# Query weights and expert rows loaded in quarters in a gated mix of an S4 convolution and a PEER mixture of experts

## The chip, the cores and the metric

One Trainium2 chip, one of its cores. The metric is the device time of one execution in microseconds; runs of one kernel are given by their median. TensorE (PE) does the matmuls, with its weight loads (PEld) beside them; VectorE (DVE), ScalarE (ACT) and GpSimd (POOL) work element by element; SyncE (SP) issues nearly all DMAs, in the order in which they stand in its program.

## What is computed

Two layers on the same 2048 tokens of 576 channels, mixed by a gate. Layer A is a long convolution, whose kernel comes from 128 complex states per channel, made by FFT; layer B picks, for each token and each of 32 heads, two of 4096 experts by the scores of two halves of a query.

```python
g = sigmoid((x * gate_w).sum(-1, keepdims=True))
K = einsum("dn,dnl,dn->dl", Cc, exp(logdA[:, :, None] * l), dB).real
a = irfft(rfft(x padded) * rfft(K padded))[:L] + x * Dskip
q = einsum("nd,dhc->nhc", x, w_q)              # 32 heads, 2 x 128
s1, s2 = q[..., :128] @ k1.T, q[..., 128:] @ k2.T   # 64 scores each
two best of s1, two best of s2 -> two best of the four sums, softmax
b = sum over heads, k of softmax * gelu(x . u[expert]) * v[expert]
out = g * a + (1 - g) * b
```

## The kernel before

The program is written out by generators that one planner interleaves. `clock[0]` is the planner's time of TensorE; `spawn` puts a generator into a heap, `yield t` asks to be resumed t microseconds later, and `pump` (line 220) resumes what is due. `rdy` holds the time at which the planner expects each tile, `dma` (line 200) adds a transfer to `wire[0]`, the time at which all transfers so far would have passed. So a `yield` is no instruction: it only decides where in the order of the engines' programs the next instruction is put. On the chip every engine runs its own list in order and waits by semaphores.

Three streams share TensorE up to the last stage. Groups `s{c}_{t}` (128 of them, 14 matmuls of 512 columns) give the scores of the 512 key columns of block c for token tile t; VectorE takes the eight best and their indices from PSUM (`scores_top`, line 952). Groups `a{c}_{tb}_{j}` (128, 14 matmuls each) give x . u for 512 experts; ScalarE or VectorE copies each to `go` and SyncE stores it to `g_d` (`act_post`, 1378). The third stream makes the convolution: `u_stage1` (1063, matmuls `u`, in 16 pieces `u1_0` to `u1_15`) transforms the input, `k_params`, `k_front`, `k_gen` (matmuls `kP`, `kb`) build the kernel K in 36 chunks; when both have ended, `freq` (1265) loads the tables `tk` and the stored chunks `ksb`, `k_stage1` (1134, matmuls `k`) and `products` (1164, matmuls `pr`, `pi`, `pv`) follow. The main loop (1725 to 1765) takes the next `s` group if its weights are there and VectorE isn't too far behind, else the next `a` group; the last 26 `a` groups are kept back as long as the next `s` block has its weights. When all groups are through, `gating` (981) gives the transposes `tr`, `prep` (1498) builds the expert weights `wh` from one-hots (matmuls `S`), and the last stage multiplies them with the values `vhl` (matmuls `o`).

Block c of the scores needs its query weights folded with the keys: `w_next` (664) loads half a block (`w_load`, tile `wq{c}_{h}`, 128 x 2304 floats, in one DMA), `w_half` (598) squares it on ScalarE, sums the squares by a matmul `wn`, folds by the matmuls `wb` and splits the result into two halves of 16 bits, `whl` and `wrem`. Block c of the experts needs `uhl`: `u_build` (1323) loads 512 expert rows by `u_load` (1309): tile `us{c}`, 128 x 4 x 512 floats, in one DMA and then the last 64 of the 576 channels twice as two short DMAs (tile `ur{c}`); `squares` (442) squares both on ScalarE and sums by a matmul `sq`, and four splits follow. Both kinds of load take the one token `raw` (`quota`, line 288) and hold it until their block is built; a second token is there from the end of `u_stage1` on.

```python
        yield from need("raw")
        take("raw", "raw")
        yield from need("slot")
        w_load(c, h)
        yield from w_half(c, h, wl[c, h])
```

Of the kernel before, what the change touches and what calls it, by code (L numbers as in the profile page):

```python
# [12 lines left out]
F32 = mybir.dt.float32  # L13
# [11 lines left out]
D = 576  # L25
# [113 lines left out]
def body(ctx: ExitStack, tc: tile.TileContext, xT, au, par, logdt, dskip, gatew, wq, kT, uT, vv,  # L139
# [17 lines left out]
    def key(x):  # L157
        n = x.tensor.name
        return (n, x.offset) if n in columns else n

    def size(x):
        n = 1
        for d in x.shape[1:]:
            n *= d
        return n
# [34 lines left out]
    def dma(o, i, q=None):  # L200
        t = max(clock[0], rdy.get(key(i), 0.0), queue[0])
        queue[0] = t + 0.45
        wire[0] = max(wire[0], t) + (2 if o.dtype in (F16, BF16) else 4) * o.shape[0] * size(o) / 3.4e5
        rdy[key(o)] = max(rdy.get(key(o), 0.0), wire[0] + 2.2)
        (q or DQ).dma_start(o, i)
# [29 lines left out]
    def ready(*xs, late=0.0):  # L235
        while True:
            t = max(rdy.get(key(x), 0.0) for x in xs) + late - clock[0]
            if t <= 0:
                return
            yield t  # L240
# [20 lines left out]
    def need(tag, n=1):  # L261
        while True:
            lst = sorted(slots[tag])
            if len(lst) >= n and lst[n - 1] <= clock[0]:
                return
            yield max(0.2, lst[n - 1] - clock[0]) if len(lst) >= n else 0.3

    def take(tag, name):
        lst = slots[tag]
        assert lst, name  # L270
        lst.remove(min(lst))

    def free(tag, *outs):
        if owed[tag]:
            owed[tag] -= 1
            return
        slots[tag].append(max([clock[0]] + [rdy.get(key(x), 0.0) for x in outs]))
# [108 lines left out]
    def slot(shape, dt, name):  # L386
        take("slot", name)
        return bp.tile([128] + shape, dt, tag="s", name=name, bufs=9)
# [35 lines left out]
    def halves_load(a, src, c):  # L424

        columns.add(a.tensor.name)
        for m in (0, 2):
            dma(a[:, m:m + 2], src[128 * m:128 * m + 256, c].rearrange("(k p) n -> p k n", p=128))
# [71 lines left out]
    def scale_first(a, r, sq, keep=None):  # L500

        acc = [newcol() for _ in range(3)]
        yield from ready(r)
        S.activation(sq[:, 4], r, AF.Square, accum_out=sc[:, acc[0]])
        for n, m in enumerate((0, 2)):
            yield from ready(a[:, m:m + 2])
            S.activation(sq[:, m:m + 2], a[:, m:m + 2], AF.Square, accum_out=sc[:, acc[n + 1]])
        yield from ready(sq)
        yield from need("kb")
        p = bank("kb", "sq")  # L510
        for n in range(3):
            mm(p[:, 0:1], onesb, short(acc[n].start, 1), n == 0, n == 2, 0.05)
        yield from ready(p)
        out = root_scale(p[:, 0:1], 1.02)
        if keep is not None:
            V.tensor_copy(keep, p[:, 0:1])
        free("kb", out[0])
        return out
# [43 lines left out]
    whl, wl, sk, halves, scaled = {}, {}, [], {}, []  # L562
    side = lambda: "kb" if caps["wb"] == 0 else "wb"

    def w_load(c, h):
        a = slot([4, D], F32, f"wq{c}_{h}")
        g = 8 * c + 4 * h
        dma(a, wq[:, g:g + 4, :])
        wl[c, h] = a
# [28 lines left out]
    def w_half(c, h, w):  # L598
        fl = lambda x: x.rearrange("p a b -> p (a b)")
        yield from ready(w)  # L600
        pbs = []
        if c == 0:
            spawn(fold_first(h, w, pbs))
        while 1 not in scaled:
            yield 0.2
        acc = newcol(True), newcol(True)
        junk = wj.tile([128, 2, D], BF16, tag="wj", name=f"wj{c}_{h}")
        for n in range(2):
            S.activation(fl(junk), fl(w[:, 2 * n:2 * n + 2]), AF.Square, accum_out=sc[:, acc[n]])
        yield from ready(junk)  # L610
        while not sk:
            yield 0.3
        tag = side()
        yield from need(tag)
        p = bank(tag, f"wn{c}_{h}")
        for n in range(2):
            mm(p[:, 0:1], onesb, short(acc[n].start, 1), n == 0, n == 1, 0.03)
        yield from ready(p)
        s, i = root_scale(p[:, 0:1], kk, True)
        V.tensor_copy(invW[:, 2 * c + h:2 * c + h + 1], i)  # L620
        free(tag, s)
        while c not in halves:
            yield 0.3
        hl, rem, count = halves[c]
        o = slice(256 * h, 256 * h + 256)
        if c:
            yield from w_fold(c, h, w, pbs, (side(),) * 3)
        while not pbs:
            yield 0.2
        for k, tag, pb in pbs:  # L630
            spawn(w_tail(c, k, pb, hl, rem, o, count, s, tag), 0.3 * k)
        del pb, pbs
        free("slot")
        if c > 0:
            free("raw")
        if h == 0 and c > 0:
            spawn(w_next(c, 1))
        elif h == 1 and c < 7:
            spawn(w_next(c + 1, 0))
# [24 lines left out]
    def w_next(c, h):  # L664
        while sdone[0] < c - (kdone[0] == NCK) and 8 * NT - len(groups) < NT * c - 5:
            yield 0.3
        yield from need("raw")
        take("raw", "raw")
        yield from need("slot")
        w_load(c, h)  # L670
        yield from w_half(c, h, wl[c, h])

    def w_build(c):
# [635 lines left out]
    def u_load(c):  # L1309
        a = slot([4, 512], F32, f"us{c}")  # L1310
        r = actp.tile([128, 512], F32, tag="ur", name=f"ur{c}")
        cs = slice(512 * c, 512 * c + 512)
        if c:
            dma(a, uT[0:512, cs].rearrange("(k p) n -> p k n", p=128))
        dma(r[0:64], uT[512:576, cs])
        dma(r[64:128], uT[512:576, cs])
        if c == 0:
            halves_load(a, uT, cs)
        return a, r

# [2 lines left out]
    def u_build(c):  # L1323
        while adone[0] < c - (kdone[0] < NCK or sdone[0] >= 7):
            yield 0.3
        if c:
            yield from need("raw")
            take("raw", "raw")
            yield from need("slot")
        a, r = xl.pop("u") if c == 0 else u_load(c)  # L1330
        if c:
            yield from ready(a, r)
        yield from need("slot")
        hl = slot([2, 4, 512], F16, f"uhl{c}")
        sq = hl.rearrange("p a k n -> p (a k) n")[:, 0:5].bitcast(BF16)
        if c == 0:
            first_u[0] = hl
            s, i = yield from scale_first(a, r, sq, nu[:, 0:1])
            marks["s"].append(1)
        else:  # L1340
            yield from squares(a, r, sq, nu[:, c:c + 1])
            s, i = root_scale(nu[:, c:c + 1], 1.02)
        if len(xb) == 4:
            V.tensor_scalar(i_a[:, c, :], i_x, i, None, op0=OP.mult)
        else:
            i_u[c] = i
        rem = wrems[c % 2]
        if c == 0:
            for k in range(4):
                S.activation(hl[:, 0, k, :], a[:, k, :], AF.Copy, scale=s)  # L1350
                marks["h"].append(S.free + 0.28)
            S.activation(rem[:, 0, :], r, AF.Copy, scale=s)
            marks["h"].append(S.free + 0.28)
        for k in range(4):
            if c:
                yield from split(hl[:, 0, k, :], hl[:, 1, k, :], a[:, k, :], s)
                continue
            while 0 not in scaled:
                yield 0.1
            rdy[key(hl)] = marks["h"][k]  # L1360
            V.scalar_tensor_tensor(hl[:, 1, k, :], a[:, k, :], s, hl[:, 0, k, :], op0=OP.mult, op1=OP.subtract)
            marks["u"].append(V.free + 0.28)
        if c:
            S.activation(rem[:, 0, :], r, AF.Copy, scale=s)
        yield from ready(rem)
        V.scalar_tensor_tensor(rem[0:64, 1, :], r[0:64], s[0:64], rem[0:64, 0, :], op0=OP.mult, op1=OP.subtract)
        if c == 0:
            marks["u"].append(V.free + 0.28)
        free("slot", hl)
        free("raw", hl)  # L1370
        uhl[c] = hl, rem
        yield from ready(rem)
        while len(scaled) < 4:
            yield 0.3
        if c < 7:
            spawn(u_build(c + 1))
# [333 lines left out]
    for w, n in ((0, 9), (1, 5)):  # L1710
        for xk in [x for k in range(4) for x in (k, 4 + k)[:2 - w]] + [8]:
            k = 4 if xk == 8 else xk % 4
            landed("x", k)
            landed("hu"[w], k)
            for j in range(4):
                cs = slice(128 * j, 128 * j + 128)
# [8 lines left out]
    while groups or acts:  # L1725
# [5 lines left out]
        if groups and bank_free() and lag < (6.0 if not a_ok else 2.0 if not turn_s else 5.0 if kdone[0] < NCK else 8.0):  # L1731
            c, t = groups[0]
# [9 lines left out]
        if acts and bank_free():  # L1742
            c, tb, j = acts[0]
# [31 lines left out]
    for t in ORDER:  # L1775
        until(lambda: t in st)
        h = st.pop(t)
# [70 lines left out]
```

## Time and profile before

| | |
|---|---|
| median of 3 runs | 1449.95 us (1448.15 to 1451.74) |
| the profiled execution | 1450.52 us, of which the span from first to last instruction 1447.6 us |
| TensorE busy | 1426.9 us, 99% |
| VectorE, ScalarE, GpSimd busy | 1208.5, 769.6, 481.5 us |
| DMA | 215.42 MB, 149 GB/s on average |
| granted TensorE clock | 1.00 |

The profile is one execution. Busy time counts an engine's instructions; a wait is put down to what ended it. Matmuls overlap, so the duration of one is longer than the step from one to the next. "issue" in the chain of waits is time in which nothing that the profile shows was waited for.

### The profile page before, as it was taken

To read this page: it belongs to the slowest core of one execution; us is meant where nothing else is said; L and a number is where in the kernel's file an instruction comes from. 1 tells how busy PE (TensorE), PEld (TensorE's weight loads), DVE (VectorE), ACT (ScalarE), POOL (GpSimd) and SP (SyncE) were. 2 spreads that over 40 slices of the span, in tenths; PEclk is the share of its full clock that TensorE was granted. 3 is DMA by queue.
4 is the path that set the end of the run, shared out by engine and by line. 5 is a ranking of instruction groups with operands and counts; after the bars stand their busy time and mean duration, and the time that the engine had idled before them with its cause. 6 is when DMAs were issued, how large, how long until landed. Compare 5 with 4: busy or idle time off the path is not lost.

```text
span 1447.6 us, 36680 instructions
## 1 busy us (share of the span) xinstructions
PE 1426.9 (99%) x14105; PEld 852.3 (59%) x14105; DVE 1208.5 (83%) x4598; ACT 769.6 (53%) x1285; POOL 481.5 (33%) x491
## 2 busy tenths in 40 slices
PE   7999999999999999999999999999999999999998
PEld 3444445455455445445555444456887887888787
DVE  6899899889877997885899897589999988888850
ACT  6346876796684776844656655655434223323310
POOL 0325357547356436220547899600000000000000
PEclk9999999999999999999999999999999999999999
DMA  8235323342324333169675777776543333342400
GB/s 308 74 117 159 96 74 120 125 143 72 117 93 150 95 105 99 49 199 293 209 272 179 255 256 270 267 259 210 196 127 111 108 120 107 123 145 68 157 10 17
DMA packets 134351, 215.42 MB, mean 149 GB/s; under 512 B 10912, under 2 KB 79904, under 8 KB 127776
## 3 DMA queue, kind: packets, MB, share of 16 engines
q1 hardware_dynamic: 134080, 213.01, 45.5%
q8 instruction: 110, 1.80, 0.5%
q14 instruction: 65, 0.53, 0.1%
q10 hardware_dynamic: 96, 0.07, 0.0%
HBM read 141.74 MB, written 71.30 MB: 147 GB/s over the span
## 4 chain that ended last, share of the span: by engine, by line
PE 89%; DMA 2%; DVE 2%; issue 0%; ACT 0%; SPq 0%; ACTq 0%; DVEq 0%
PE o L214 26%; PE s L214 24%; PE a L214 23%; PE S L214 4%; PE kb L214 2%; PE pr L214 2%; PE wb L214 2%; PE y L214 1%; PE kP L214 1%; PE pv L214 1%; PE u L214 1%; PE k L214 1%; DMA z_d<-vo 1%; DMA ksb<-k_d 1%; DVE i L134 1%; DMA vn<-in_au_dram 0%
## 5 line engine op out<-in xcount | busy, mean ns | idle before, releaser
L214 PE MATMUL o<-vhl,wh 128*128 128x288 f16 x3072 | 387.0, 286 | 0.0
L214 PE MATMUL s<-whl,xb 128*128 128x512 f16 x1536 | 363.9, 379 | 0.0
L214 PE MATMUL a<-xb,uhl 128*128 128x512 f16 x1536 | 359.7, 379 | 0.2 <-DVE go L134 0.2
L214 PEld LDWEIGHTS <-wh 128*128 128x128 f16 x3072 | 296.0, 98 | 76.3 <-issue 3.7
L214 PEld LDWEIGHTS <-xb 128*128 128x128 f16 x1792 | 170.6, 98 | 210.1 <-issue 15.3
L214 PEld LDWEIGHTS <-uhl 128*128 128x128 f16 x1536 | 147.3, 98 | 176.2 <-issue 3.4
L134 DVE FIND_INDEX8 i<-m,s 128x8 uint32<-128x64 f32 x1024 | 206.5, 222 | 0.0
L134 ACT ACTIVATE wh<-gl,s_wg 128x1024 f16<-128x1024 f32 x64 | 68.9, 1137 | 202.3 <-DVE gl L134 202.3
L134 DVE MAX8 m<-s 128x8 f32<-128x64 f32 x1024 | 146.3, 215 | 29.3 <-PE s L214 28.4
L134 POOL TENSOR_TENSOR CS<-CS,ex 128x512 f32<-128x512 f32 x72 | 98.0, 1393 | 147.6 <-DVE ex L134 146.2
L134 ACT ACTIVATE go<-a,i_a 128x512 f32<-128x512 f32 x94 | 63.2, 685 | 96.4 <-PE a L214 68.6
L134 DVE TENSOR_TENSOR gl<-S,gl 128x256 f32<-128x256 f32 x256 | 90.5, 416 | 12.6 <-PE S L214 8.3
L134 POOL TENSOR_TENSOR e<-aN,rt 128x512 f32<-128x512 f32 x72 | 83.2, 1177 | 49.9 <-PE kb L214 43.7
L134 DVE SCALAR_TENSOR_TENSOR wh<-gl,s_wg,wh 128x1024 f16<-128x1024 f32 x63 | 78.6, 1280 | 10.7 <-ACT wh L134 10.7
L134 DVE TENSOR_TENSOR Bg<-Be,vals 128x1024 f16<-128x1024 f16 x128 | 84.6, 702 | 2.2
L134 ACT ACTIVATE gl<-gl 128x1024 f32<-128x1024 f32 x64 | 63.5, 1045 | 34.2 <-DMA gl<-g_d 31.1
L134 DVE TENSOR_TENSOR A<-iota_a,vals 128x2048 f16<-128x2048 f16 x64 | 77.9, 1216 | 0.0
L214 PE MATMUL s<-wrem,xb 128*128 128x512 f16 x256 | 76.2, 379 | 0.0
L214 PE MATMUL a<-xb,wrem 128*128 128x512 f16 x256 | 75.9, 379 | 0.0
L214 PEld LDWEIGHTS <-A 128*128 128x128 f16 x2048 | 70.5, 97 | 4.7
L134 DVE MATCH_VALUE_LOAD i<-m,s 128x8 f32 x1024 | 72.6, 71 | 0.1
L214 PE MATMUL S<-Bg,A 128*128 128x64 f16 x2048 | 72.3, 193 | 0.0
(205 smaller groups left out, 2068.5 us busy)
## 6 DMA issues: line engine op xcount, KB each, us to landing
g_d<-go SPq DMA_DIRECT2D x128, 256.0 KB, 2.5
gl<-g_d SPq DMA_DIRECT2D x32, 1024.0 KB, 5.4
wq<-in_wq_dram SPq DMA_DIRECT2D x16, 1152.0 KB, 6.0
su_d<-us SPq DMA_DIRECT2D x32, 288.0 KB, 2.6
sk_d<-k1o SPq DMA_DIRECT2D x32, 288.0 KB, 2.9
ui<-su_d SPq DMA_DIRECT2D x16, 576.0 KB, 4.0
ki<-sk_d SPq DMA_DIRECT2D x16, 576.0 KB, 5.3
vn<-in_vv_dram SPq DMA_DIRECT2D x32, 288.0 KB, 5.4
```

What stands on the lines that cost most here:

```text
L134: return f(*a, **k)
L214: T.matmul(o, l, r, start=start, stop=stop)
```

## The change

Each load of query weights behind the first block, and each load of expert rows behind the first block, is put out as four DMAs of a quarter, with `yield 1.5` behind each, before the generator goes on. For the expert rows the two short DMAs of the last 64 channels go first. The loads of the first blocks stay as they were.

```diff
@@ w_next
         yield from need("slot")
-        w_load(c, h)
+        a = wl[c, h] = slot([4, D], F32, f"wq{c}_{h}")
+        for j in range(4):
+            dma(a[:, j], wq[:, 8 * c + 4 * h + j, :])
+            yield 1.5
         yield from w_half(c, h, wl[c, h])
@@ u_load
         cs = slice(512 * c, 512 * c + 512)
-        if c:
-            dma(a, uT[0:512, cs].rearrange("(k p) n -> p k n", p=128))
-        dma(r[0:64], uT[512:576, cs])
-        dma(r[64:128], uT[512:576, cs])
         if c == 0:
+            dma(r[0:64], uT[512:576, cs])
+            dma(r[64:128], uT[512:576, cs])
             halves_load(a, uT, cs)
         return a, r
@@ u_build
         a, r = xl.pop("u") if c == 0 else u_load(c)
+        if c:
+            cs = slice(512 * c, 512 * c + 512)
+            dma(r[0:64], uT[512:576, cs])
+            dma(r[64:128], uT[512:576, cs])
+            for k in range(4):
+                dma(a[:, k], uT[128 * k:128 * k + 128, cs])
+                yield 1.5
         if c:
             yield from ready(a, r)
```

How the order moves. First SyncE at the first load of expert rows behind the first block (`us1`, `ur1`; `us_909` and `us_912` are the input of `u_stage1`, and a name's last number is only its place in the program), before:

```order
L205 DMA g_d_65<-go0_2_2_765 128x4x128
L205 DMA us1_790<-in_uT_dram 128x4x512
L205 DMA ur1_791<-in_uT_dram 64x512 x2
L205 DMA us_909<-in_au_dram 64x576
L205 DMA us_909<-in_au_dram 64x1x576
L205 DMA tu0_916<-in_tu_dram 128x256
L205 DMA us_909<-in_au_dram 64x1x576 x2
L205 DMA tu1_1032<-in_tu_dram 128x256
```

and now:

```order
L205 DMA g_d_65<-go0_2_2_765 128x4x128
L205 DMA ur1_791<-in_uT_dram 64x512 x2
L205 DMA us1_790<-in_uT_dram 128x512 x4
L205 DMA us_912<-in_au_dram 64x576
L205 DMA us_912<-in_au_dram 64x1x576
L205 DMA tu0_919<-in_tu_dram 128x256
L205 DMA us_912<-in_au_dram 64x1x576 x2
L205 DMA tu1_1035<-in_tu_dram 128x256
```

The short rows stand ahead of four quarters, and nothing stands between these. Second, SyncE where `tk` and `ksb` are loaded (`su_d`: stores of `u_stage1`; `k_d`: the stored chunks of K; `wq5_0`, `wq5_1`: weights of block 5), before:

```order
L205 DMA g_d_65<-go6_0_0_7904 128x4x128
L205 DMA su_d_66<-us_909 32x4x576 x2
L205 DMA k_d_68<-ko_8040 128x1024
L205 DMA wq5_0_8151<-in_wq_dram 128x2304
L205 DMA tk0_8166<-in_tk_dram 128x4096
L205 DMA tk16_8167<-in_tk_dram 128x4096
L205 DMA ksb_8162<-k_d_68 128x18x256
L205 DMA g_d_65<-go6_0_1_8288 128x4x128
L205 DMA ksb_8162<-k_d_68 128x18x256
L205 DMA wq5_1_8341<-in_wq_dram 128x2304
L205 DMA g_d_65<-go6_0_2_8352 128x4x128
L205 DMA g_d_65<-go6_0_3_8378 128x4x128
```

and now:

```order
L205 DMA g_d_65<-go7_0_0_7866 128x4x128
L205 DMA wq5_0_7926<-in_wq_dram 128x576 x2
L205 DMA g_d_65<-go7_0_1_7935 128x4x128
L205 DMA wq5_0_7926<-in_wq_dram 128x576
L205 DMA tk0_7974<-in_tk_dram 128x4096
L205 DMA tk16_7975<-in_tk_dram 128x4096
L205 DMA g_d_65<-go7_0_2_7978 128x4x128
L205 DMA wq5_0_7926<-in_wq_dram 128x576
L205 DMA ksb_7970<-k_d_68 128x18x256 x3
L205 DMA wq5_1_8169<-in_wq_dram 128x576
L205 DMA ksb_7970<-k_d_68 128x18x256
L205 DMA wq5_1_8169<-in_wq_dram 128x576 x3
```

The store ahead of these loads was that of group `a6_0_0` and is now that of `a7_0_1`; the `ksb` were one by one between stores, and now three stand together; two loads of weights are cut up among them. Third, ScalarE at the last piece of `u_stage1` and the last `kb` (chunk `kb34`), before:

```order
L134 ACTIVATE us_909<-u1_15_0_0_7944 128x288
L134 ACTIVATE us_909<-u1_15_0_1_7946 128x288
L134 ACTIVATE us_909<-u1_15_1_0_7945 128x288
L134 ACTIVATE us_909<-u1_15_1_1_7947 128x288
L134 ACTIVATE ko_8040<-kb34_7968 128x512
L134 ACTIVATE uhl7_7918<-us7_7873,sci_76 128x512 x3
```

and now:

```order
L134 ACTIVATE ko_7557<-kb34_7485 128x512
L134 ACTIVATE wj4_0_7595,sc_75<-wq4_0_7409 128x1152 x2
L134 ACTIVATE vals_80<-m8_3_8_7369 128x4x16
L134 ACTIVATE idx_117<-i8_3_8_7370 128x4x16
L134 ACTIVATE uh15_7667<-us_912,sci_76 128x576
L134 ACTIVATE whl4_7706<-wb4_0_0_7707,sci_76 128x2x256
L134 ACTIVATE whl4_7706<-wb4_0_2_7708,sci_76 128x2x256
L134 ACTIVATE wrem2_116<-wb4_0_4_7709,sci_76 64x128 x4
L134 ACTIVATE go6_1_2_7793<-a6_1_2_7765,i_a_91 128x512
L134 ACTIVATE vals_80<-m8_3_12_7602 128x4x16
L134 ACTIVATE idx_117<-i8_3_12_7603 128x4x16
L134 ACTIVATE us_912<-u1_15_0_0_7810 128x288
```

The copies of `u1_15` stood right ahead of that of `kb34`, and now they stand behind it, with a load of weights for block 4, its split and a store's `go` between.

## Rows read from the trace of the kernel before

**Rows 1.** The page, busy us, share of the span and instructions of each engine.

```profile
PE 1426.9 (99%) x14105; PEld 852.3 (59%) x14105; DVE 1208.5 (83%) x4598; ACT 769.6 (53%) x1285; POOL 481.5 (33%) x491
```

**Rows 2.** Waits of TensorE: who, for whom, us in total, times, longest us.

```profile
PE sq L214 <- ACT xb L134: 9.0, 3, 5.0
PE sq L214 <- ACT uhl L134: 1.8, 1, 1.8
PE k L214 <- ACT k1o L134: 1.5, 1, 1.5
PE kb L214 <- issue: 1.5, 1, 1.5
```

**Rows 3.** Chain of waits in order of time: start us, us, matmuls.

```profile
150.82 6.04 PE a L214 x28
```

**Rows 4.** DMA issues of the whole span: count, KB each, median us to landing.

```profile
wq<-in_wq_dram SPq DMA_DIRECT2D x16, 1152.0 KB, 6.0
su_d<-us SPq DMA_DIRECT2D x32, 288.0 KB, 2.6
vn<-in_vv_dram SPq DMA_DIRECT2D x32, 288.0 KB, 5.4
```

**Rows 5.** Instructions on tile wq: the issues on SyncE, ns minimum, median, maximum.

```profile
L205 SPq DMA_DIRECT2D wq<-in_wq_dram x16: 345/431/2457, 8.7 to 771.1; - x16
```

**Rows 6.** Timeline, 62 to 102 us: start us, us, engine; idle before, releaser.

```profile
73.52 0.67 SPq L205 DMA_DIRECT2D us<-in_uT_dram  x1
74.24 1.53 SPq L205 DMA_DIRECT2D ur<-in_uT_dram  x2
80.88 1.91 ACT L134 ACTIVATE uhl<-us 128x2048 bf16<-128x2048 f32 x1 [2.90 <-DMA us<-in_uT_dram]
...
83.55 0.16 PE L214 MATMUL sq<-sc,onesb 128*128 128x2 bf16 x1 [1.77 <-ACT uhl L134]
```

**Rows 7.** Timeline of TensorE around the last u and the first k.

```profile
633.33 0.91 PE L214 MATMUL u<-uh,tu 64*128 64x288 f16 x12
...
680.04 1.39 PE L214 MATMUL k<-ksb,tk 128*128 128x288 f16 x10 [0.61 <-DMA ksb<-k_d]
```

**Rows 8.** Timeline of SyncE, 618 to 760 us.

```profile
644.30 0.81 SPq L205 DMA_DIRECT2D tk<-in_tk_dram  x2
...
671.96 0.67 SPq L205 DMA_DIRECT2D ksb<-k_d  x1
```

**Rows 9.** Window 645 to 650 us (last two: DMA share, GB/s); DMA of 640 to 690 us.

```profile
645.00:650.00 5.00, 5.00 (x25) 2.25 (x23) 4.86 (x33) 3.37 (x6) 0.00 (x0) 1.00 0.98 379
...
DMA packets 7824, 14.17 MB, mean 283 GB/s; under 512 B 448, under 2 KB 4032, under 8 KB 7179
```

**Rows 10.** The page, costliest groups: busy us, mean ns of one, idle before.

```profile
L134 DVE FIND_INDEX8 i<-m,s 128x8 uint32<-128x64 f32 x1024 | 206.5, 222 | 0.0
...
L134 DVE MAX8 m<-s 128x8 f32<-128x64 f32 x1024 | 146.3, 215 | 29.3 <-PE s L214 28.4
...
L134 ACT ACTIVATE go<-a,i_a 128x512 f32<-128x512 f32 x94 | 63.2, 685 | 96.4 <-PE a L214 68.6
...
L134 DVE MATCH_VALUE_LOAD i<-m,s 128x8 f32 x1024 | 72.6, 71 | 0.1
```

**Rows 11.** Window 679 to 934 us: busy us of PE, PEld, DVE, ACT, POOL.

```profile
679.00:934.00 255.00, 251.88 (x2275) 127.07 (x2273) 214.93 (x1348) 147.91 (x403) 183.31 (x248) 1.00 0.73 247
```

**Rows 12.** Timeline of VectorE in the tail, 895 to 1030 us.

```profile
938.20 0.29 DVE L134 CAST iota_a<-cst 128x256 f16<-128x256 f32 x1 [6.83 <-ACT vals L134]
...
949.38 0.94 DVE L134 TENSOR_TENSOR vals<-tr,vals 128x64 f16<-128x64 f32 x4 [2.24 <-ACT vals L134]
...
993.36 1.28 DVE L134 SCALAR_TENSOR_TENSOR wh<-gl,s_wg,wh 128x1024 f16<-128x1024 f32 x1
```

**Rows 13.** Timeline of TensorE in the tail: first transposes, first matmuls o.

```profile
933.58 0.31 PE L214 MATMUL tr<-identb,vals 128*64 128x64 bf16 x4
...
995.77 11.92 PE L214 MATMUL o<-vhl,wh 128*128 128x288 f16 x96
```

## The prediction

> **What bounds the kernel now.** First I read the busy time of each engine [rows 1]: TensorE 1426.9 of 1447.6 us, VectorE 1208.5, the others far less. A gain can only come out of the 20.7 us in which TensorE was idle. Then what TensorE waited for [rows 2]: 9.0 us are three waits on ScalarE's `xb` at the start, before the first weights are there, which the change doesn't touch; the longest after them are 1.8, 1.5 and 1.5 us. To be sure that "busy" hides no idling, I read the pitch of the matmuls in the chain of waits [rows 3]: 28 matmuls of 512 columns in 6.04 us, 0.216 us each. At 2.4 GHz, the clock granted in that stretch, this is hardly more than one column per cycle. One group of 14 matmuls (`s` or `a`) is thus 3.02 us.
>
> The Trainium skill (Perfetto Trace Analysis, Identifying the Most-Contended Engine) calls matmul busy time a poor measure of how near TensorE is to its limit and asks for the share of the weight loads, which is 59% here [rows 1]: by that rule a good part of the span would be open. The pitch speaks against it, and the sum below goes by the pitch.
>
> **The change, part by part.** No matmul and no size changes. Each load of query weights behind the first block (14 of 1152 KB) and of expert rows (7 of 1024 KB) becomes four DMAs: 63 more on SyncE, 0.431 us each [rows 5], 27 us in all on an engine that TensorE's longest waits don't name [rows 2], and at most 3 x 0.431 = 1.3 us in one load. The pause of 1.5 us is a step of the planner's clock; no instruction waits for it. The order shows the first load's four quarters back to back. A quarter is held back only where another instruction, mostly a store that waits for its `go`, stands between. What the pause does is move the order: the planner keeps the one `raw` token longer and hands it out in another sequence, and all that stands before the `o` stage is shuffled.
>
> (1) *Landing.* A whole load of weights lands 6.0 us after its issue; a transfer of a quarter's size 2.6 us after it in quiet stretches (`su_d`) and 5.4 in busy ones (`vn`) [rows 4]. The last quarter thus lands 1.3 + 2.6 to 5.4 = 3.9 to 6.7 us after the first issue, -2.1 to +0.7 us beside now. It costs only where somebody waits. In the new order I counted the work on TensorE between the `a` group whose store stands ahead of a last quarter and the matmul that sums the squares of that load. The least is 8.8 us for weights (`wq4_1`: 37 long matmuls and one piece of `u`) and 9.0 us for expert rows (the last load). Under it lie the `go` copy, 0.69 us [rows 10], two issues, 0.9 us, the landing, 2.6 to 5.4 us, and the squares, 2.7 us (from 80.88 to 83.55, [rows 6]): 6.9 to 9.7 us. Quiet stretches are nearer, since these loads fall before 630 us. Cost 0, bounds 0 and +2 (two loads, 0.7 to 0.9 us each).
>
> (2) *The one load whose lateness shows before:* the first expert rows. Issued at 73.52, ScalarE began their squares at 80.88, and TensorE stood 1.77 us at `sq` [rows 6]. Now three more matmuls stand ahead of `sq` (0.65 us gained), but the two short rows go first (their issues took 1.53 us [rows 6]) and three issues come on top (1.3 us). Bounds: -1.8 us, if the rows land in time, and 1.53 + 1.3 - 0.65 = +2.2 us, if the last quarter lands as much later as it is issued. I take the middle, 0.
>
> (3) *The hand-over to the second stage of the K transform.* Before, the last piece of `u` stood ahead of the last `kb`; now it stands far behind it, and only after it may `tk` and `ksb` be loaded. Before, that piece ended at 634.2 and TensorE got the last `ksb` at 680.04, after a wait of 0.61 us [rows 7]; it was issued at 671.96 [rows 8]. Now 148 long matmuls stand between that piece and the first `k`, 32.0 us, and two folds of weights of some 2.25 us: 36.5 us of cover instead of 45. Below it: store `go7_0_1` stands ahead of `tk`, and its group is through after 8.8 us; with the `go` copy and the issues `tk` goes out at 10.4 us. From there to the last `ksb` 7.67 MB are to be moved (two `tk` of 1.05, four `ksb` of 1.18, a store, two quarters). At 379 GB/s, a full stretch [rows 9], this takes 20.2 us, at the 283 GB/s of the whole 50 us around it 27.1 us: landed at 30.6 or 37.5 us. The four `ksb` no longer stand apart behind stores, so the full stretch is nearer: cost 0. Bounds: -0.6 us (the old wait gone) and +9.6 us (35.7 us from `tk`'s issue at 644.30 to the landing as before, behind 10.4 us, less the cover).
>
> (4) *The balance of `s` and `a`.* Weights come later now: 71 `s` groups instead of 80 stand ahead of the first `k` matmul, and 107 `a` instead of 104. An `s` costs VectorE (206.5 + 146.3 + 72.6) / 128 = 3.32 us [rows 10], more than its 3.02 us on TensorE. From the first `k` matmul to the first transpose now stand 56.6 instead of 48.0 `s`: 28.6 us more of VectorE, and with 1.6 more `a` and one fold 33 us more of TensorE. Before, VectorE was busy 215 of 255 us there [rows 11], 84%; now 243.5 of 288, 85%. Hidden, 0. The stage ahead gets shorter by what this one grows.
>
> (5) *The tail.* From the first transpose to the first `o` matmul stand 165 instead of 230 `a` matmuls and 6 instead of 8 blocks of `S`: 46 us instead of the 62 from 933.58 to 995.77 [rows 13]. Under it VectorE makes the first weights `wh`. It began at 938.20, 4.6 us after the first transpose, and its last `wh` started at 993.36 [rows 12], 56.4 us in all. Of this the new order moves behind that `wh` two one-hots (6.1 us), eight products with `S` (2.8) and one pair of `vhl` (1.5), and puts a `go` (0.75) ahead: 46.8 us. With a start 1.5 us after the transpose 48.3 us; less its wait of 2.24 us on ScalarE [rows 12], 46.1. Cost 0, bounds 0 and +5 (start as late as before).
>
> **Sum.** 1450.52 us of the profiled execution (span 1447.6 and 2.9 around it) and five times 0. It lies 0.57 above the median of the runs, so 1449.95, say **1450.0**. The bounds together: -2.4 and +18.8.
>
> The Trainium skill (DMA: Bandwidth & Descriptors, Measured) asks to batch DMAs to 1 MiB or more, and puts about 2 us of fixed cost on each; it speaks against this change. No row of before shows quarters of one load; by that figure, an estimate, a load would end 3 x 2 = 6 us later. Worked out from rows instead, this is rival C.
>
> **Rivals.**
> A, *slower: TensorE waits for `ksb`* at its first `k`. It decides from a rate below 7.67 MB / 26.1 us = 294 GB/s. For it: TensorE waited there already, with 9 us more of cover. Against: 379 GB/s. Price up to 9.6 us: 1459.6.
> B, *faster: the new order closes gaps* [rows 2]. The planner reckons a load to land later than before and puts its consumers later. Against: only the 1.8 us at `sq` hang on such a load. Price -5 us of all that is listed behind the start: 1445.
> C, *slower: the quarters land one behind another*, 4 x 5.4 = 21.6 us. With 2.7 us of squares five loads of weights miss their cover (15 to 20 us from the first quarter on) by 4 to 10 us, together 33: 1483. Against: two `tk` issued in 0.81 us were moved at 379 GB/s [rows 8, 9].
> D, *slower: VectorE becomes the bound* where `s` is now dense, 17.7 instead of 10 groups in the second half of the products: 17.7 x 0.30 = 5.3 us, 1455.3. Against: 85%.
> E, *the change doesn't do what it says*: no pause on the chip, only an order. The same time; it is part of the forecast.
>
> **Chances.** Forecast with E 0.71, A and its like in the tail 0.14, B 0.09, D 0.04, C 0.02. A measurement of this kernel can tell about 0.3%, 4.35 us, from no change. Faster 0.09 (B), same 0.71, slower 0.20 (A, C, D). The range takes in A, D and B, and leaves out C and several bounds falling together: 1445 to 1460.
>
> **What would show it.** Right: TensorE busy 1427 us again and idle within 4 us of 20.7; quarters 0.4 to 0.6 us apart where nothing stands between; `sq` behind a wait of 0 to 4 us, and no wait over 1 us for `wq` or `us` elsewhere. A is a wait of several us of `k` on the DMA of `ksb`, C landing times that climb by 5 us from quarter to quarter, D VectorE busy throughout between 800 and 930 us. I'm wrong if TensorE's idle time grows by over 4 us at a place that I counted as covered.

## The result and the profile after

The changed kernel takes 1452.88 us (median of 22 runs, 1451.11 to 1455.95) beside 1450.55 (22 runs, 1446.61 to 1453.84): 1.0017 of the time before, 95% interval 1.0010 to 1.0025. That is within 0.3%, as forecast, but it is a small loss and not nothing. The profiled execution took 1452.79 us, its span is 1450.9.

The busy line of the page, which answers to [rows 1]:

```profile
PE 1427.4 (98%) x14103; PEld 851.9 (59%) x14105; DVE 1227.3 (85%) x4617; ACT 755.6 (52%) x1268; POOL 479.2 (33%) x490
```

TensorE works as long as before (1426.9 us) and is idle for 1450.9 - 1427.4 = 23.5 us instead of 20.7. Its waits, which answer to [rows 2] (who, for whom, us in total, times, longest us):

```profile
PE sq L214 <- ACT xb L134: 9.5, 3, 5.1
PE k L214 <- DVE i L134: 2.9, 2, 1.5
PE k L214 <- ACT k1o L134: 2.3, 3, 1.6
PE u L214 <- DVE uh L134: 1.7, 2, 1.4
PE sq L214 <- ACT uhl L134: 1.3, 1, 1.3
PE wn L214 <- ACT wj L134: 0.6, 1, 0.6
```

Two lines matter. By the profile's names stage `k` now waits 2.9 us for VectorE's indices of the scores (`i`), which it didn't before, and 2.3 us for `k1o` instead of 1.5. The wait of `kb` (1.5) has shrunk to two of 0.2 us, and one of `pv` (1.0) is gone. The timeline of TensorE puts the waits of `k` in two places:

```profile
621.54 0.91 PE L214 MATMUL u<-uh,tu 64*128 64x288 f16 x12
...
659.73 0.41 PE L214 MATMUL k<-ksb,tk 128*128 128x288 f16 x2
...
661.64 0.41 PE L214 MATMUL k<-ksb,tk 128*128 128x288 f16 x2 [1.50 <-DVE i L134]
...
709.64 0.71 PE L214 MATMUL k<-ksb,tk 128*128 128x288 f16 x4 [1.58 <-ACT k1o L134]
...
712.51 0.41 PE L214 MATMUL k<-ksb,tk 128*128 128x288 f16 x2 [0.35 <-ACT k1o L134]
...
714.64 0.65 PE L214 MATMUL k<-ksb,tk 128*128 128x288 f16 x4 [0.37 <-ACT k1o L134]
...
717.32 0.66 PE L214 MATMUL k<-ksb,tk 128*128 128x288 f16 x4 [1.39 <-DVE i L134]
```

The first stands right behind the hand-over, the others at the end of the stage. At the first, the name `i` is not what TensorE waited for. This matmul waits for several semaphores, and the profile names the last one that it saw. The index that VectorE wrote just ahead of it is the second of the eight of its group:

```profile
661.38 0.22 DVE L134 FIND_INDEX8 i<-m,s 128x8 uint32<-128x64 f32 x1
...
662.58 0.22 DVE L134 FIND_INDEX8 i<-m,s 128x8 uint32<-128x64 f32 x1
```

VectorE reads the bank of a group of scores up to its eighth index, and that came at 662.58, when `k` was running. But this pair of matmuls is also the first that reads the last of the four `ksb`. That one was issued at 652.60 and landed 8.9 us later, at 661.50:

```profile
652.60 0.66 SPq L205 DMA_DIRECT2D ksb<-k_d  x1
DMA to landing us min/median/max: 8.9/8.9/8.9
```

TensorE starts 0.14 us behind this landing. Before, where the profile does name `ksb` [rows 7], it also started 0.14 us behind the landing of the last one. So the 1.50 us are a wait for `ksb`, and before they were 0.61. The expectations of the later runs still go by the name `i`. The 1.39 us at 717.32 do end with VectorE's indices.

Together 1.50 + 1.58 + 0.35 + 0.37 + 1.39 = 5.2 us, where before stood 0.61 + 1.50 = 2.1 us. In 1451 us that is all that the change costs in this stage (`ksb` +0.9, `k1o` +0.8, `i` +1.4), and with the small differences elsewhere it is the whole loss: `k` +3.1, the start +0.5, `wn` +0.6, `u` +0.7, `s` +0.4, against `kb` -1.0, `pv` -1.0 and the first `sq` -0.5, in sum +2.8 us, the growth of TensorE's idle time.

A quarter lands 4.4 us after its issue, between the 2.6 and the 5.4 that were taken as bounds; the row of DMA issues that answers to [rows 4] (count, KB each, median us to landing):

```profile
wq<-in_wq_dram SPq DMA_DIRECT2D x56, 288.0 KB, 4.4
```

And the first expert rows, which answer to [rows 6]:

```profile
73.33 1.51 SPq L205 DMA_DIRECT2D ur<-in_uT_dram  x2
74.93 1.97 SPq L205 DMA_DIRECT2D us<-in_uT_dram  x4
80.91 1.91 ACT L134 ACTIVATE uhl<-us 128x2048 bf16<-128x2048 f32 x1 [3.08 <-DMA us<-in_uT_dram]
83.58 0.16 PE L214 MATMUL sq<-sc,onesb 128*128 128x2 bf16 x1 [1.29 <-ACT uhl L134]
```

Four quarters are issued in 1.97 us, 0.49 each, back to back; ScalarE starts at 80.91 where it started at 80.88.

### The profile page after: what moved, and what is told of

It reads as the page before. It is cut to its first block, busy times and chain, and to the rows that moved or that the text cites. A ratio compares the mean times of both kernels' runs of the same rounds, so it can differ in the third digit from the quotient of the medians.

```text
span 1450.9 us, 36774 instructions
## 1 busy us (share of the span) xinstructions
PE 1427.4 (98%) x14103; PEld 851.9 (59%) x14105; DVE 1227.3 (85%) x4617; ACT 755.6 (52%) x1268; POOL 479.2 (33%) x490
## 4 chain that ended last, share of the span: by engine, by line
PE 85%; DVE 5%; ACT 1%; DMA 1%; issue 0%; POOL 0%; SPq 0%; DVEq 0%; ACTq 0%
PE o L214 26%; PE a L214 23%; PE s L214 20%; PE S L214 4%; PE kb L214 2%; PE wb L214 2%; PE pr L214 2%; DVE i L134 2%; DVE m L134 1%; PE y L214 1%; PE kP L214 1%; PE pv L214 1%; DMA sk_d<-k1o 1%; PE u L214 1%; PE k L214 1%; ACT CS L134 0%
## 5 line engine op out<-in xcount | busy, mean ns | idle before, releaser
L134 ACT ACTIVATE go<-a,i_a 128x512 f32<-128x512 f32 x74 | 49.7, 682 | 76.2 <-PE a L214 48.9
L134 DVE MATCH_VALUE_LOAD i<-m,s 128x8 f32 x1024 | 69.1, 67 | 0.2
```

The source lines that it names most:

```text
L134: return f(*a, **k)
```

## The experiments

The change does two things at once: it cuts transfers, and it makes the planner write another order. The first experiments take these apart.

**The cut in the old order.** The planner books one whole load, but four DMAs are put out. All engines but SyncE run the very order of before.

```diff
-        (q or DQ).dma_start(o, i)
+        for po, pi in parts or [(o, i)]:
+            (q or DQ).dma_start(po, pi)
...
-        dma(a, wq[:, g:g + 4, :])
+        dma(a, wq[:, g:g + 4, :], parts=[(a[:, j], wq[:, g + j, :]) for j in range(4)] if c else None)
```

(and the same for the expert rows; the short rows stay behind them)

> The 21 loads go as four DMAs each, but the planner books each as one transfer, so the order of all other instructions is that of the kernel before. Theory O (the order alone makes the time): the time of before, ratio 0.999 to 1.001, and TensorE's waits behind the start add up to 8 us as in before, sq about 1.8 us. Theory S (the cut loads cost by themselves, by 63 more issues and later landings): ratio 1.001 to 1.0025, with new waits at sq, wn or k.

Measured: 1447.6 us, ratio 0.9983 (0.9974 to 0.9992), 2.4 us *faster*, a little below what theory O allowed and against theory S. Three of its waits of TensorE, in the columns of [rows 2]; behind the start there are only two more, at `u` and `a`:

```profile
PE sq L215 <- ACT uhl L134: 1.3, 1, 1.3
PE kb L215 <- issue: 0.9, 1, 0.9
PE k L215 <- ACT k1o L134: 0.9, 1, 0.9
```

The waits for `ksb` and at `pv` are not there, those at `kb`, `k1o` and `sq` are each about 0.5 us shorter. Cutting costs nothing; in this order it even gives a little.

**The new order without the cut.** Planner, pauses and places as in the change, but the first quarter's DMA carries the whole load and the other three are not put out.

```diff
             dma(a[:, j], wq[:, 8 * c + 4 * h + j, :],
+                real=[] if j else [(a, wq[:, 8 * c + 4 * h:8 * c + 4 * h + 4, :])])
             yield 1.5
```

(and the same for the expert rows)

> The planner books and pauses as in the changed kernel, but each load goes as one whole DMA at the place of its first quarter, so the order of all other instructions is that of the changed kernel. Theory O: the time of the changed kernel, ratio 1.001 to 1.0025, with the same four or five waits of k (5 us in all). Theory S: the time of before, ratio 0.999 to 1.001, k waits 2 us or less, since no quarters stand among the stores of k1o.

Measured: 1454.27 us, ratio 1.0028 (1.0017 to 1.0039). This is just above theory O's range, and far from theory S. So the loss is in the order, some 4 us of it, and the quarters seem to give about 1.5 us of it back (1.0017 against 1.0028, with intervals that overlap). Two of its waits:

```profile
PE k L215 <- ACT k1o L134: 2.0, 1, 2.0
PE k L215 <- DMA ksb<-k_d: 1.8, 1, 1.8
```

With whole loads the first `k` waits 1.8 us for `ksb`, with quarters 1.5. In this order `ksb` comes late either way, and the smaller pieces take at most 0.3 us off that.

**One half of the change alone.** Weights cut and paused, expert rows as before; then the other way round.

```diff
@@ w_next only
+        for j in range(4):
+            dma(a[:, j], wq[:, 8 * c + 4 * h + j, :])
+            yield 1.5
```

> Only the loads of query weights are cut and paused; the expert rows as before. Its order is a third one. Theory O: any ratio from 0.998 to 1.003, to be read from its own waits; TensorE's idle time and the median move together. If the lateness of the weights is the cause (s groups pushed up to the first k), then as the changed kernel, 1.001 to 1.0025, with waits of k on VectorE; the variant with expert rows alone then as before.

```diff
@@ u_load, u_build only
+            dma(r[0:64], uT[512:576, cs])
+            dma(r[64:128], uT[512:576, cs])
+            for k in range(4):
+                dma(a[:, k], uT[128 * k:128 * k + 128, cs])
+                yield 1.5
```

> Only the loads of expert rows are cut and paused, with the short rows first; the weights as before. Theory O: any ratio from 0.998 to 1.003, again by its own waits. If the weights are the cause: 0.999 to 1.001 and no wait of k on VectorE. The wait at the first sq as in the changed kernel, 1.3 us.

Measured: 1477.15 us, ratio 1.0175 (1.0153 to 1.0197), for the weights, and 1487.53 us, 1.0254 (1.0235 to 1.0274), for the expert rows. Each half alone costs more than ten times as much as both together, far outside the 0.998 to 1.003 that was expected of any order. The three largest waits of the first that are new or have grown:

```profile
PE k L214 <- DMA ksb<-k_d: 4.8, 1, 4.8
PE S L214 <- DVE Bg L134: 3.4, 4, 2.0
PE a L214 <- issue: 3.0, 1, 3.0
```

and those of the second:

```profile
PE o L214 <- DVE vhl L134: 9.0, 6, 3.4
PE S L214 <- DVE Bg L134: 4.8, 6, 2.6
PE wn L214 <- ACT wj L134: 4.5, 2, 3.4
```

None of these is the landing of a cut load. The nearest is `wn` on `wj`, the squares of the weights; the weights are whole in the second kernel, and in the first, where they are cut, this wait is 1.6 us. The others are at places that the change doesn't name, the values `vhl` in the `o` stage above all.

**Both halves again with whole DMAs**, each with its own order kept, by the edit shown for the new order without the cut:

> The order of the kernel with paused weights alone (1477.15 us), but each load of weights is one whole DMA at the place of its first quarter. Theory O (the order costs): about the same, 1472 to 1482 us, ratio to the kernel before 1.015 to 1.022, with stalls of TensorE again behind 1000 us at S and a granted clock under 1 in places. Rival T (quarters that stand among other loads come late): back to 1450 to 1456 us, since the first DMA now carries all four quarters.

> The order of the kernel with paused expert rows alone (1487.53 us), but the rows go as one whole DMA at the place of their first quarter, the short ones still first. Theory O: 1482 to 1493 us, ratio 1.022 to 1.030, with the waits of o and S on VectorE between 1000 and 1065 us as before. Rival T: 1450 to 1456 us.

Measured: 1475.33 us, ratio 1.0169 (1.0148 to 1.0191), and 1485.76 us, 1.0242 (1.0222 to 1.0262). The intervals overlap with those of the cut loads. The 25 and 36 us are the order's, whatever the loads look like.

**The cut without the pause, and twice the pause.** Four DMAs each and the short rows first, with the line `yield 1.5` left out, and then with

```diff
-            yield 1.5
+            yield 3.0
```

> Both loads in quarters and the short rows first, as in the change, but the planner doesn't pause behind a quarter. Theory O (the order costs, not the quarters): without the pause the order stays near that of before, 80.0 groups of scores ahead of the first k matmul instead of 71.4, and in front of it stand expert groups instead of four groups of scores. So the 1.50 us that TensorE stood at k for VectorE in the change are gone, and most of the 2.3 us for k1o: 1446 to 1450 us, ratio to the kernel before 0.997 to 1.000. Rival T (the quarters and the short rows first cost something themselves, the pause nothing): about as the change, 1452.9 us, ratio 1.0017, with waits of TensorE behind the start over 9 us in all.

> The change with a pause of 3.0 instead of 1.5 us behind each quarter: 6 us more in which a load holds its token. Theory O: the length of the pause has no price of its own. The order built with it has 71.6 groups of scores ahead of the first k and four of them right in front of it, as in the change, so k waits 1.5 us for VectorE again: 1451 to 1456 us, unless a load or a buffer comes late where the order no longer covers it, as in the kernel with paused weights alone (then 20 to 35 us more, with a stall of over 3 us and a fallen granted clock behind it). Rival P (each load that is held longer delays its block): the change's cost doubles with the pause, 1455 to 1460 us, in waits at sq and wn, with no stall of over 3 us.

Measured: 1451.86 us, ratio 1.0013 (1.0004 to 1.0023), without, and 1474.98 us, 1.0171 (1.0153 to 1.0189), with the longer pause. Without the pause, theory O missed: the kernel isn't as fast as the cut in the old order. Rival T had the time, but its reason falls with the runs before and after this one, in which neither the cut nor the short rows ahead of it cost anything. Four bookings in place of one already give another order, without any pause; in it TensorE waits 2.6 us at `k` for VectorE (`i`) and 2.0 at `S` for `Bg`, at places that neither theory named. The longer pause shows 9.9 us of `S` on `Bg`, the longest 5.7, and 6.9 of `wn` on `wj`, the longest 4.8: stalls of over 3 us, against rival P, which wanted none. The wait that theory O put at the first `k` is 0.3 us; the time is that of its exception, a late place that the order no longer covers. 0, 1.5 and 3.0 us of pause thus give 1451.9, 1452.9 and 1475.0; no price per microsecond fits that.

**Six buffers for `k1o`** in place of four, in the change and then in the cut with the old order. No engine's order moves.

```diff
-            o = fk.tile([128, D], F32, tag="s1o", name=f"k1o{w}", bufs=4)
+            o = fk.tile([128, D], F32, tag="s1o", name=f"k1o{w}", bufs=6)
```

> The change with six buffers for k1o instead of four, the order of all engines as in the change. Theory B (stage k stands still because a k1o buffer comes free only when its store has landed, behind the quarters of weights): the waits of k on k1o (1.58, 0.35 and 0.37 us) go, and VectorE's wait on the stores with the 1.39 us behind it too; 2.3 to 3.7 us less than the change: 1449.2 to 1450.6 us, ratio to the kernel before 0.999 to 1.000. Rival V (VectorE is behind there, since 7.4 groups of scores stand right ahead of the first k): the same time moves to k's wait on VectorE, 1452.5 to 1453.3 us.

> The loads cut in four in the order of the kernel before (1447.6 us), and six buffers for k1o instead of four. Theory B: k's only wait there, 0.88 us on k1o, goes: 1446.7 us, ratio to the kernel before 0.9977. Rival: the wait was for a store that is late anyway, and the next one that needs it waits: 1447.6 us, 0.9983.

In the change: 1451.76 us, ratio 1.0012 (1.0002 to 1.0022), 1.1 us less than the change: between the two theories, and not told apart from no change by the intervals. In stage `k` theory B is right: the waits on `k1o` are gone, and so is the 1.39 us for `i`. What is left is 1.2 us at the pair that reads the last `ksb`; the profile calls it `m`, and it again ends 0.14 us behind the last sign of `ksb`'s semaphore. The trace also shows why the gain is so small. A wait of 1.1 us at `wn` is new, and the old one there is 0.8:

```profile
PE wn L214 <- ACT wj L134: 1.9, 2, 1.1
PE k L214 <- DVE m L134: 1.2, 1, 1.2
```

TensorE reaches the next block's weights earlier, and these aren't squared yet. In the old order: 1445.7 us, ratio 0.9972 (0.9962 to 0.9982), a little more than theory B's value gives, faster than before and than the change by more than the intervals, and 1.9 us under the same cut with four buffers, where the intervals overlap. Stage `k` no longer waits, and behind the start these two waits are the longest:

```profile
PE u L215 <- DVE uh L134: 1.8, 2, 1.4
PE sq L215 <- ACT uhl L134: 1.2, 1, 1.2
```

**The short rows first**, added to this last kernel, and **only the weights cut**, in the old order with four buffers:

```diff
             dma(a, uT[0:512, cs].rearrange("(k p) n -> p k n", p=128),
+                real=[(r[0:64], uT[512:576, cs]), (r[64:128], uT[512:576, cs])]
+                + [(a[:, k], uT[128 * k:128 * k + 128, cs]) for k in range(4)])
```

> The loads cut in four in the order of the kernel before, six buffers for k1o (1445.7 us), and now the two short DMAs of each load of expert rows ahead of its quarters; nothing else moves. If the quarters' landing counts for the first block of rows, which are the ones waited for, the wait at sq near 83 us grows from 1.2 us by up to the 1.5 us of the two issues: up to 1447.2 us, ratio to the kernel before 0.997 to 0.998. If the last to land is a short row, the wait shrinks by as much: down to 1444.5 us, 0.9962. The prediction's middle: no change, 1445.7 us.

> Only the loads of weights are cut in four, the expert rows stay whole, all in the order of the kernel before, four buffers for k1o. Both cut gave 1447.6 us, none 1450.0. If the gain comes from stage k, where quarters of weights stand among ksb and the stores of k1o (its waits there 0.61 and 0.62 us shorter) and from z stores at 918 us: 1447.6 to 1448.3 us, ratio 0.998 to 0.999. If it comes from the expert rows (sq at 83 us 0.5 us shorter, and what lies beside them): 1449.2 to 1450.0 us, ratio 0.9995 to 1.

Measured: 1444.93 us, ratio 0.9965 (0.9952 to 0.9978), with the wait at `sq` 1.7 instead of 1.2 us: nothing that the intervals tell from no change. With the weights alone cut: 1450.21 us, ratio 0.9997 (0.9986 to 1.0009), no gain, against the first of the two values expected. The `ksb` wait of before (0.6) is gone here too; three others are those of before:

```profile
PE k L215 <- ACT k1o L134: 1.7, 1, 1.7
PE kb L215 <- issue: 1.6, 1, 1.6
PE pv L215 <- ACT vo L134: 1.3, 1, 1.3
```

This points to the cut of the expert rows for the 2.4 us, alone or beside that of the weights, though the intervals of the two kernels overlap and no kernel with the rows alone cut in this order was run. One of the three waits that were shorter with both cut stands next to such a load: TensorE stops at `kb` ("issue") some 6 us after a load of expert rows was issued at 448 us, for 1.50 and 1.59 us where that is one DMA, 0.95 us where it is four, and not at all in the two kernels of this order with four DMAs and six buffers. The shorter wait at `sq` is not the rows' doing, since it is 1.3 us with whole rows too. How `k1o` and `pv` hang on the rows stays open.

## Why the prediction was right, and where it wasn't

The forecast of no change held: 1452.88 against 1450.0, ratio 1.0017. "TensorE idle within 4 us of 20.7" holds with 23.5. But the five zeros weren't all zeros. A wait that the working had at nothing and one that it left out added some 3 us, and gains of 2 us at `kb` and `pv` that it didn't count took most of that back. That part is luck.

(1) *Landing*: right. Only one load shows, 0.6 us at `wn`. The pairs that differ in nothing but the cut say it without the order: 0.9983 against 1; 1.0017 against 1.0028; 1.0175 against 1.0169; 1.0254 against 1.0242. Cutting is worth between -0.2% and +0.1%, in four orders, and in three of the four the intervals overlap. Rival C is refuted. The Trainium skill (DMA: Bandwidth & Descriptors, Measured), with its 1 MiB for a DMA (measured there on DMAs issued from GpSimd), spoke against the cut; these pairs show no loss by it, since TensorE hardly waits for these loads.

(2) *First expert rows*: right. The wait at `sq` is 1.29 us instead of 1.77, and the kernel with whole rows and only the weights cut has 1.33. So the half microsecond isn't owed to the cut of the rows.

(3) *Hand-over*: here the step failed, by little. The cover was right: `tk` was issued 10.7 us behind the last piece of `u` (10.4 were reckoned), and the cover is 659.73 - 622.45 = 37.3 us (36.5). The landing was not. The last `ksb` landed 661.50 - 622.45 = 39.1 us behind that piece, later than both values of the working, 30.6 and 37.5. From the issue of `tk` to that landing more was moved than the 7.67 MB that were reckoned:

```profile
DMA packets 4498, 9.03 MB, mean 319 GB/s; under 512 B 214, under 2 KB 1215, under 8 KB 4238
```

The rate of 319 GB/s lies between the 283 and 379 of the working, so the term that was too small is the amount. It left out what was issued just ahead of `tk` and the three quarters of weights just behind the last `ksb`. Rival A is thus what happened: the 7.67 MB took 28.3 us, which is 271 GB/s and under its 294. Its price was 1.5 us, 0.9 more than before, and not the 9.6 at its upper end.

(4) *Balance of `s` and `a`*: right that it costs nothing. From the first `k` to the first transpose VectorE was busy 252.3 of 291.2 us, 87% (85% were reckoned), and between 800 and 930 us TensorE had no idle time at all. The price of 3.32 us for an `s` was too high, since it adds up durations that overlap. Early among the 7.4 groups `s` in a row ahead of the first `k` VectorE starts one every 3.02 us and stands 0.28 us of that, so one costs it 2.74:

```profile
641.12 1.15 DVE L134 MAX8 m<-s 128x8 f32<-128x64 f32 x8 [0.28 <-PE s L214]
...
644.14 1.15 DVE L134 MAX8 m<-s 128x8 f32<-128x64 f32 x8 [0.28 <-PE s L214]
```

*A term that was missing*: `k1o`. [Rows 2] showed 1.5 us there, and the text left it as it is. In the change the stores of `k1o` share SyncE with the quarters of block 6 at 702 to 709 us:

```profile
702.14 0.36 SPq L205 DMA_DIRECT2D wq<-in_wq_dram  x1
702.61 0.52 SPq L205 DMA_DIRECT2D sk_d<-k1o  x1
703.18 0.58 SPq L205 DMA_DIRECT2D wq<-in_wq_dram  x1
703.87 0.52 SPq L205 DMA_DIRECT2D sk_d<-k1o  x1
```

and VectorE, which empties the banks of `k`, waits for one of them to land:

```profile
714.16 0.46 DVE L134 COPY k1o<-k 128x288 f32<-128x288 f32 x1 [4.16 <-DMA sk_d<-k1o]
```

Behind this stop VectorE's indices are late too, and TensorE waits the 1.39 us for them. That buffers are the link is shown by six of them (no wait on `k1o` left in stage `k`, in both orders, and no 1.39 us). That the quarters among the stores make it longer is not shown: with whole loads the same place has one wait of 2.0 us.

(5) *Tail*: right to half a microsecond. 46 us were reckoned from the first transpose to the first `o`, and with six blocks of `S` in front VectorE starts the last `wh` just in time:

```profile
950.92 0.31 PE L214 MATMUL tr<-identb,vals 128*64 128x64 bf16 x4
...
997.36 1.88 PE L214 MATMUL o<-vhl,wh 128*128 128x288 f16 x14
```

The last `wh` ahead of it begins at 996.04 and TensorE doesn't wait. With other orders it waits later in the `o` stage, by 9.0 us for `vhl` in the kernel with the rows alone.

Rival B was right in part: `kb` and `pv` lost 2.0 us of waits, which the stage `k` took back. D didn't come: VectorE was busy 115 of the 130 us from 800 to 930, and TensorE never waited for it there. E was right more deeply than meant: on the chip the pause is only an order, and the order is all that costs. That either half alone costs 27 or 38 us also says that the forecast's 0.71 rested on having read this very order; for "some other order" it would have been far too sure.

## What to carry to other kernels

Where a planner writes the order, run a change twice before believing in its reason: its order with the old instructions, and its instructions in the old order. With an engine at 98% the price of an order is a handful of waits of 1 to 5 us, so read the 10 to 20 us in front of each consumer (what load it reads, who must have emptied its bank, whose store must have landed) and not the busy share of a stage. In a reckoning of when a load lands, count what is issued just ahead of it and just behind it as well. And where an instruction waits for several semaphores, look up when each was ready before believing the name in the profile: here "VectorE" stood for a DMA that had landed 0.14 us earlier. The version to keep here is the cut in the old order with two more `k1o` buffers, 0.9972.

## What the runs showed of the hardware that was not expected

**A stall can also cost the clock.** In the kernel with paused weights alone TensorE stood 4.84 us for `ksb` until 701.16. In windows of 5 us (PE, PEld, DVE, ACT, POOL, granted clock, DMA share, GB/s):

```profile
695.00:700.00 5.00, 1.32 (x7) 0.48 (x5) 0.00 (x0) 0.99 (x2) 0.00 (x0) 0.98 1.05 321
700.00:705.00 5.00, 3.84 (x14) 2.09 (x15) 0.92 (x2) 0.82 (x2) 0.00 (x0) 0.50 1.01 338
705.00:710.00 5.00, 5.00 (x27) 2.60 (x25) 3.40 (x25) 3.15 (x7) 0.00 (x0) 0.84 0.53 176
710.00:715.00 5.00, 5.00 (x29) 2.51 (x28) 3.96 (x33) 1.27 (x4) 0.95 (x1) 1.00 0.65 160
```

Behind it the matmuls ran at 0.50, 1.2 GHz, until past 705. Over the whole execution TensorE was busy 1435.8 us for the work that took 1426.9 before: 8.9 of the 25.7 us of longer span are not idle time but longer busy time, and the matmuls at half the clock are at least a part of that. The change and its twin with whole loads differ in it at the same place. First the twin, with one wait of 2.02 us that ended at 710.84:

```profile
710.00:712.00 2.00, 1.16 (x5) 0.61 (x5) 1.63 (x12) 1.62 (x6) 0.21 (x1) 0.71 1.02 380
712.00:714.00 2.00, 2.00 (x7) 0.96 (x7) 2.00 (x16) 1.50 (x5) 1.94 (x4) 0.50 0.92 307
```

then the change, with four shorter ones and 3.69 us in all:

```profile
710.00:712.00 2.00, 2.00 (x14) 1.21 (x13) 0.00 (x1) 0.71 (x2) 1.88 (x3) 1.00 1.03 350
712.00:714.00 2.00, 1.65 (x10) 0.77 (x8) 0.00 (x0) 0.71 (x2) 1.18 (x4) 1.00 0.86 310
```

Its clock stayed at 1.00. So the twin's 2.02 us of wait and 1429.0 - 1427.4 = 1.6 us of longer busy time came to as much as 3.69 us of idling in pieces. The length of a stall alone doesn't decide it: the twin's 1.84 us for `ksb`, which ended at 662.89, left the clock at 1.00, while in the kernel with the longer pause two stalls of 1.57 and 1.84 us, which ended at 189.80 and 192.25, were followed by 0.50 from 193 to 196 us. What does decide it is not shown here. The Trainium skill (TensorE: Matmul & The Clock Gate, Part 1: The HAM clock gate) says that activity releases a throttle that is on by default; the drop behind the stall agrees with it.

**An issue can take much longer than its median.** Three issues of `ksb` took 11.67 us together in the change, where one took 0.67 before [rows 8]:

```profile
636.43 11.67 SPq L205 DMA_DIRECT2D ksb<-k_d  x3
```

The first took 0.75 us, the others 5.89 and 4.13, behind the two `tk` (issued at 633.16), a store and a quarter of weights; the next quarter took 4.19. The DMA engines were busy throughout (share 1.02 to 1.06 from 636 to 660 us, at 291 to 397 GB/s). In the twin with whole loads the three took 10.97 us, so the quarters are not the reason; that the issues wait for what is on the way is likely, but no run shows it. In such a stretch a sum that takes 0.43 us for an issue is too short.
